# A new order for the pieces of a windowed-attention stage, a minimum for the sink columns, and sink remainders on GpSimd

## The chip, the cores and the metric

The kernel runs on one core of a Trainium2 chip. A time is the device time of one execution in microseconds (us); the kernel before has a median of 281.07 us over three runs (279.21, 281.07 and 281.68). Five engines work side by side, each through its own queue in program order: TensorE (PE) multiplies and transposes, VectorE (DVE), ScalarE (ACT) and GpSimd (POOL) work on tiles, and SyncE (SP) mostly starts transfers (DMA). An instruction that waits for another engine holds up everything behind it in its own queue.

## The reference

Three stages follow one another. The change is in the first one.

```python
def _attn_ref(q, k, v, n_sink, window):          # 4 batches, 8 heads, 768 tokens, 64 wide
    scores = scale * np.matmul(q, k.transpose(0, 1, 3, 2))
    keep = (pos[None, :] < n_sink) | ((rel >= 0) & (rel < window))   # n_sink = 4, window = 128
    scores = np.where(keep, scores, -1000000000.0)
    a = np.exp(scores - np.max(scores, axis=-1, keepdims=True))
    a = a / (np.sum(a, axis=-1, keepdims=True) + 1e-09)
    return np.matmul(a, v)
...
x = _moe_ref(...)     # a soft mixture of 8 experts over the 3072 tokens
return _moe2_ref(...) # each token through its one best expert
```

A token attends to the 128 tokens up to itself and to the first four tokens, the sink. All data are 32-bit floats.

## The kernel before, in words

**Units.** Two heads form a pair; there are 16 pairs. A pair has six blocks of 128 tokens and is worked in three units of two blocks, so there are 48 units. A unit u goes through twelve pieces, each a function `emit_...`:

- S (PE, L220): scores of two blocks for two heads into one of two PSUM tiles `sc0`, `sc1`. The tile of unit u is free again when E of unit u-2 has read it.
- M (DVE, L235): one predicated copy that folds the previous block's keys into the window. L (DVE, L243, L244): the row maximum; in a pair's first unit also L246, which puts the sink columns of the first block out of play by a predicated copy of `negs` under the mask `m_dup`.
- E (ACT, L257): four exponentials with row sums. R (DVE, L262, L263): the reciprocals. N (POOL, L267): the normalization.
- G (POOL, L275 to L277): the sink probabilities into the tile `st`, as a rounded part and a remainder. T (PE, L286): four transposes. C (ACT, L291): out of PSUM. A, B, D (POOL, L297 to L304): the triangles of the window into `pt`.

**Pairs.** A pair also has its own pieces: v0 (ACT, L310) rounds the sink values of `v` into `vst`, and v1 (DVE, L315) puts their remainder beside it; s and k (PE L320, DVE L326) spread the sink probabilities; P0 to P8 (PE, L333 to L341) multiply by `v`, into `xa` and `xb`; x (ACT, L346, L348) brings the result to SBUF; X, y, f and l transpose it, store it by token in `xtok` (ACT, L375) and add up the next stage's logits. After every fourth pair, eight more steps (among them L405 and L417 on PE) fold a finished batch into the mixture.

**Transfers.** SP's queue starts a pair's loads of `qk` (L80, two buffers: pair p waits for the last S of pair p-2) and `v` (L85, three buffers: a load waits until the last P of an earlier pair has read its buffer), and between them the weights of the next stage, 1 MB at a time (L488).

**What sets the order.** Every piece gets a number, its unit plus a key from the table `KEYS` (by the piece's name, the pair modulo four, and the first and last pair), and the pieces are written out in the order of these numbers. Each engine's queue, SP's too, follows that order; the waits between engines come from the data and the buffers alone. The stages after attention, from L530 on, have an order of their own, and the change does not touch it.

Of the kernel before, what the change touches and what calls it, by code (L numbers as in the profile page):

```python
# [33 lines left out]
NX = 10  # L34
CAP = 128 + NX
NEG = -1.0e30


@with_exitstack
def kernel_body(ctx, tc, qkv, n_sink, window, phi, m1w, emb, tau, m2w1, m2w2, out):  # L40
# [71 lines left out]
    pool.affine_select(out=t_le_q, in_=ones, pattern=[[-1, 128]], compare_op=ALU.is_ge, fill=0.0, base=0, channel_multiplier=1)  # L112

    m_dup = const.tile([128, 2, 2, SINK], F32, name="m_dup")
    ov = ones[:, 0:8].rearrange("p (h s) -> p h s", h=2)
    pool.affine_select(out=m_dup[:, :, 0, :], in_=ov, pattern=[[0, 2], [-1, SINK]], compare_op=ALU.is_ge, fill=0.0, base=0, channel_multiplier=1)
    pool.affine_select(out=m_dup[:, :, 1, :], in_=ov, pattern=[[0, 2], [1, SINK]], compare_op=ALU.is_gt, fill=0.0, base=0, channel_multiplier=-1)
    negs = const.tile([128, 16], F32, name="negs")
    dve.memset(negs, NEG)

    bm = const.tile([96, 4], F32, name="bm")
    for c in range(3):
# [65 lines left out]

    emit_W(5)
    dve.memset(sc_b[1], 0.0)  # L190
    dve.memset(negs, NEG)
    s_t, p_t, pt_t, xt_t, xtok_b = {}, {}, {}, {}, {}
    rs_t, nm_t = {}, {}

# [42 lines left out]
    def emit_L(u):  # L237
        p, t = divmod(u, 3)
        mv = merged(s_t[u])
        nm = small.tile([128, 2, 2], F32, tag="nm", name="nm")  # L240

        mx = mv[:, :, :, 192]
        dve.tensor_reduce(mx, mv[:, :, :, 0:UW], axis=X, op=ALU.max, negate=True)  # L243
        dve.tensor_scalar(out=nm, in0=mx, scalar1=0.125, scalar2=None, op0=ALU.mult)  # L244
        if t == 0:
            dve.copy_predicated(mv[:, :, :, 128:UW], m_dup.bitcast(U32), negs.rearrange("p (h i s) -> p h i s", h=2, i=2))  # L246
        nm_t[u] = nm

    def emit_E(u):
# [62 lines left out]

    def emit_v1(p):
        vst = vst_t[p]
        dve.tensor_tensor(out=vst[64:96, :], in0=v_t[p][64:96, VW:], in1=vst.bitcast(F32)[64:96, :], op=ALU.subtract)  # L315

    def emit_s(p, half):
        if half == 0:
# [70 lines left out]
    def dispatch(b):  # L389
# [37 lines left out]
    NU = 3 * NPAIR  # L427
    wx = ExitStack()
    KEYS = {
# [41 lines left out]
    }  # L471
    n_exp, n_done = {}, {}
    disp = {}
# [1180 lines left out]
```

## Time and profile before

| | us |
|---|---|
| median of three runs | 281.07 |
| profiled execution, its own time | 281.05 |
| its span, first to last instruction | 279.3 |
| attention, first S to last f | 5.9 to 162.3 |

Busy time over the span: PE 262.2 us (94%), DVE 194.1 (69%), ACT 193.4 (69%), POOL 162.0 (58%). TensorE's granted clock is 0.993 of full speed on average. In the profile, a line gives a group of like instructions with their busy time and the mean length of one in ns; an "idle before" is time in which the engine had nothing to run before that instruction, with the instruction that ended the wait. A busy PE is modelled from the starts of pipelined matmuls, so it also contains their fill and drain.

### The profile page before, as it was taken

The page shows a single profiled execution, that of the slowest core. Times are in us where ns is not written, and L with a number is a line of the kernel's source. Part 1 is how long each engine was busy: PE and PEld are TensorE (multiplying, and loading weights), DVE is VectorE, ACT ScalarE, POOL GpSimd, SP SyncE. Part 2 cuts the span into 40 slices and gives each one's busy share as a digit, 9 for nine tenths or more (in the row PEclk, how much of TensorE's full clock was granted, in tenths as well). Part 3 has the DMA queues.
Part 4 walks back from the last instruction along what each step waited for, and adds up shares of the span by engine and source line. Part 5 has one row for each costly group of instructions (what it writes and reads, how often), then busy time and mean ns, then how long its engine had stood idle before and what let it go on. Part 6 is the DMA issues. An engine that isn't in the chain of part 4 may idle for free.

```text
span 279.3 us, 8848 instructions
## 1 busy us (share of the span) xinstructions
PE 262.2 (94%) x3257; PEld 166.3 (60%) x3257; DVE 194.1 (69%) x574; ACT 193.4 (69%) x679; POOL 162.0 (58%) x377
## 2 busy tenths in 40 slices
PE   7988999979999989999999999999999998999990
PEld 5654666555666655666556663334387675677880
DVE  6887888997878998789987243444435989664410
ACT  2677989869799797898987632310135999686981
POOL 3488999978889888899888640001202996020000
PEclk9999999999999999999999999999999999999997
DMA  7939976199383596768616398999139200025874
GB/s 222 329 123 409 391 281 220 19 402 392 93 314 118 204 419 260 277 235 310 253 82 228 111 408 333 427 429 419 60 123 393 87 1 1 2 75 137 313 284 175
DMA packets 15197, 65.37 MB, mean 234 GB/s; under 512 B 2736, under 2 KB 3248, under 8 KB 11568
## 3 DMA queue, kind: packets, MB, share of 16 engines
q1 hardware_dynamic: 13600, 63.77, 60.7%
q10 hardware_dynamic: 1392, 0.48, 0.8%
q8 instruction: 27, 0.44, 0.6%
q0 software_dynamic: 160, 0.52, 0.6%
q14 instruction: 18, 0.15, 0.2%
HBM read 58.48 MB, written 6.29 MB: 232 GB/s over the span
## 4 chain that ended last, share of the span: by engine, by line
PE 57%; DVE 16%; POOL 10%; DMA 6%; issue 5%; ACT 4%; SPq 0%; POOLq 0%; ACTq 0%; DVEq 0%
PE sc L220 5%; PE b L858 5%; POOL pr L267 5%; PE m L286 4%; PE xa L341 4%; PE b L834 4%; DVE sc L243 3%; PE b L1195 3%; PE b L1385 3%; PE m L358 3%; PE xb L341 3%; DMA out_dram<-ot 2%; PE m L365 2%; DVE sc L235 2%; PE m L417 2%
## 5 line engine op out<-in xcount | busy, mean ns | idle before, releaser
L257 ACT ACTIVATE pr<-sc,nm 128x132 f32<-128x132 f32 x192 | 68.7, 375 | 8.5 <-DVE rs L262 3.4
L267 POOL TENSOR_TENSOR pr<-pr,rs 128x528 f32<-128x528 f32 x48 | 51.5, 1073 | 21.3 <-DVE rs L263 16.4
L257 ACT ACTIVATION_READ_ACCUMULATOR pr<-sc,nm 128x1 f32 x192 | 40.4, 210 | 0.0
L220 PE MATMUL sc<-qk 64*32 64x164 f32 (+4 forms) x1536 | 36.6, 294 | 0.3 <-ACT pr L257 0.2
L235 DVE COPY_PREDICATED sc<-t_le_q,sc 128x512 f32<-128x512 uint32 x48 | 33.1, 689 | 3.6 <-PE sc L220 2.3
L291 ACT ACTIVATE raw<-m 128x512 f32<-128x512 f32 x48 | 29.0, 604 | 7.9 <-PE xb L320 4.3
L243 DVE TENSOR_REDUCE sc<-sc 128x4 f32<-128x528 f32 x48 | 33.7, 703 | 0.8
L286 PE MATMUL m<-ident,pr 128*128 128x128 f32 x192 | 30.2, 280 | 3.9 <-ACT xtok L375 2.8
L297 POOL TENSOR_SCALAR_AFFINE_SELECT pt<-raw 128x512 f32<-128x512 f32 x48 | 30.6, 638 | 1.9 <-ACT raw L291 1.9
L341 PE MATMUL xa<-pt,v 128*64 128x256 f32 (+1 forms) x256 | 30.3, 360 | 0.0
L286 PEld LDWEIGHTS m<-ident,pr 128*128 128x128 f32 x192 | 21.4, 141 | 12.0 <-POOL pr L267 4.3
L220 PEld LDWEIGHTS sc<-qk 64*32 64x32 f32 x1536 | 21.2, 106 | 10.5 <-issue 4.4
L341 PEld LDWEIGHTS xa<-pt,v 128*64 128x64 f32 x256 | 15.4, 136 | 8.4 <-issue 4.3
L813 POOL CAST scr<-scr 128x256 fp32r<-128x256 f32 x6 | 2.4, 402 | 30.7 <-DVE scr L809 30.0
L304 POOL TENSOR_SCALAR_AFFINE_SELECT pt<-raw 128x256 f32<-128x256 f32 x48 | 19.6, 408 | 0.0
L341 PE MATMUL xb<-pt,v 128*64 128x128 f32 (+1 forms) x192 | 18.9, 314 | 0.0
L1172 POOL TENSOR_TENSOR w2h<-w2t,ones 128x512 fp32r<-128x512 f32 x8 | 8.3, 1043 | 15.4 <-PE b L1022 15.4
L375 ACT ACTIVATE xtok<-m 128x512 f32<-128x512 f32 (+1 forms) x32 | 15.7, 499 | 2.0 <-PE m L358 1.7
L341 PEld LDWEIGHTS xb<-pt,v 128*64 128x64 f32 x192 | 11.6, 136 | 7.3 <-POOL st L277 2.5
L358 PE MATMUL m<-ident,xt 128*128 128x128 f32 x96 | 15.9, 276 | 0.0
L1204 ACT ACTIVATE junk<-b 128x512 f32<-128x512 f32 (+1 forms) x26 | 14.8, 568 | 0.7 <-PE b L1195 0.3
L1385 PE MATMUL b<-w2c,hm 128*128 128x512 f32 x45 | 14.7, 400 | 0.0
(328 smaller groups left out, 571.2 us busy)
## 6 DMA issues: line engine op xcount, KB each, us to landing
w<-in_m1w_dram SPq DMA_DIRECT2D x19, 1024.0 KB, 8.2
qk<-in_qkv_dram SPq DMA_DIRECT2D x15, 780.0 KB, 4.4
w<-in_m1w_dram SPq DMA_DIRECT2D x4, 2048.0 KB, 12.8
v<-in_qkv_dram SPq DMA_DIRECT2D x16, 448.0 KB, 4.9
out_dram<-ot SPq DMA_DIRECT2D x19, 256.0 KB, 2.9
x<-in_m1w_dram SPq DMA_DIRECT2D x4, 1024.0 KB, 8.5
w1t<-in_m2w_dram SPq DMA_DIRECT2D x4, 512.0 KB, 5.2
w2t<-in_m2w_dram SPq DMA_DIRECT2D x4, 512.0 KB, 8.9
```

The costliest lines, as they stand in the source:

```text
L220: pe.matmul(sc[r0:r0 + 32, h, o + lo:o + hi], lhsT=lhsT, rhs=qk[hp:hp + 64, k0 + lo:k0 + hi], start=True, stop=True)
L235: dve.copy_predicated(mv[:, :, :, 0:128], mk.to_broadcast([128, 2, 2, 128]), bv[:, :, :, 124:252])
L243: dve.tensor_reduce(mx, mv[:, :, :, 0:UW], axis=X, op=ALU.max, negate=True)
L257: act.activation(out=pr[:, h, i2, :], in_=mv[:, h, i2, 0:UW], func=AF.Exp, bias=nm[:, h, i2:i2 + 1], scale=0.125, accum_out=sm[:, h, i2, 0:1])
L267: pool.tensor_tensor(out=pr, in0=pr, in1=sm.rearrange("p h (i o) -> p h i o", o=1).to_broadcast([128, 2, 2, UW]), op=ALU.mult)
L286: pe.transpose(ps[:, h, i2, :], pr[:, h, i2, 0:128], ident)
L291: act.activation(out=raw, in_=tp_t.pop(u), func=AF.Copy)
L297: pool.affine_select(out=pt[:, :, :, 0, :], in_=raw_t[u], pattern=[[0, 2], [0, 2], [1, 128]], compare_op=ALU.is_ge, fill=0.0, base=0, chan ...
L304: pool.affine_select(out=pt_t[u][:, :, 0, 1, :], in_=raw_t[u][:, :, 1, :], pattern=[[0, 2], [-1, 128]], compare_op=ALU.is_gt, fill=0.0, ba ...
L341: pe.matmul(o[64 * h:64 * h + 64, c0:c0 + 128 * (l1 - l0)], lhsT=v[:, j, h, :], rhs=mv[:, h, 128 * l0:128 * l1], start=False, stop=last, s ...
L358: pe.transpose(ps[:, 128 * t:128 * t + 128], xt[:, 128 * (t0 + t):128 * (t0 + t) + 128], ident)
L1385: pe.matmul(y, lhsT=a, rhs=b, start=(k == 0), stop=(k == 3))
```

## The change

Three edits. (1) `KEYS` has new numbers, so pieces, and loads among them, stand in another order on every engine. (2) The tile `m_dup` no longer holds 0 and 1 but -1e30 where a sink column is to be masked and 3e38 elsewhere, and a `tensor_tensor` with `min` takes the place of the predicated copy; `negs` and its two memsets are gone, and POOL gets one memset. (3) v1 goes from DVE to POOL. The number of matmuls, of other instructions and of loads is otherwise the same.

```diff
+BIG = 3.0e38
...
     m_dup = const.tile([128, 2, 2, SINK], F32, name="m_dup")
-    ov = ones[:, 0:8].rearrange("p (h s) -> p h s", h=2)
-    pool.affine_select(out=m_dup[:, :, 0, :], in_=ov, pattern=[[0, 2], [-1, SINK]], compare_op=ALU.is_ge, fill=0.0, base=0, channel_multiplier=1)
...
-    negs = const.tile([128, 16], F32, name="negs")
-    dve.memset(negs, NEG)
+    pool.memset(m_dup, NEG)
+    pool.affine_select(out=m_dup[:, :, 0, :], in_=m_dup[:, :, 0, :], pattern=[[0, 2], [-1, SINK]], compare_op=ALU.is_ge, fill=BIG, base=0, channel_multiplier=1)
...
-            dve.copy_predicated(mv[:, :, :, 128:UW], m_dup.bitcast(U32), negs.rearrange("p (h i s) -> p h i s", h=2, i=2))
+            dve.tensor_tensor(out=mv[:, :, :, 128:UW], in0=mv[:, :, :, 128:UW], in1=m_dup, op=ALU.min)
...
-        dve.tensor_tensor(out=vst[64:96, :], in0=v_t[p][64:96, VW:], in1=vst.bitcast(F32)[64:96, :], op=ALU.subtract)
+        pool.tensor_tensor(out=vst[64:96, :], in0=v_t[p][64:96, VW:], in1=vst.bitcast(F32)[64:96, :], op=ALU.subtract)
...
-        "T@3": (2.984, 2.2177, 1.8544,), "C@3": (3.2592, 2.8973, 2.1591,), ...
+        "T@3": (2.5712, 2.2359, 2.0133,), "C@3": (3.0669, 2.2451, 2.1058,), ...
```

What the numbers do is seen in the queues. Three places, each before and then with the change. The number behind a tile's name only tells tiles of one name apart.

**Place A, SP's queue near its start, before.** `qk_277` and `qk_286` are the loads of pairs 2 and 3, `v_102`, `v_296` and `v_344` those of pairs 1, 2 and 3.

```order
L85 DMA v_102<-in_qkv_dram 128x896
L488 DMA w0_273<-in_m1w_dram 128x2048
L80 DMA qk_277<-in_qkv_dram 128x1560
L80 DMA qk_286<-in_qkv_dram 128x1560
L85 DMA v_296<-in_qkv_dram 128x896
L488 DMA w0_273<-in_m1w_dram 128x2048
L488 DMA w1_320<-in_m1w_dram 128x2048
L85 DMA v_344<-in_qkv_dram 128x896
```

The same place with the change: `qk_270` and `qk_276` are pairs 2 and 3, `v_273` is pair 3 and `v_278` pair 2.

```order
L86 DMA v_102<-in_qkv_dram 128x896
L485 DMA w1_232<-in_m1w_dram 128x2048
L485 DMA w0_237<-in_m1w_dram 128x2048 x2
L81 DMA qk_270<-in_qkv_dram 128x1560
L86 DMA v_273<-in_qkv_dram 128x896
L81 DMA qk_276<-in_qkv_dram 128x1560
L86 DMA v_278<-in_qkv_dram 128x896
```

Three weight loads instead of one now stand ahead of pair 2's `qk`, the third `v` load follows it at once, and pair 3's `qk` no longer stands between.

**Place B, SP's queue at pairs 6 and 7, before.** `qk_606` and `v_891` are pair 6, `qk_810` and `v_1026` pair 7.

```order
L80 DMA qk_606<-in_qkv_dram 128x1560
L80 DMA qk_810<-in_qkv_dram 128x1560
L85 DMA v_891<-in_qkv_dram 128x896
L488 DMA w2_582<-in_m1w_dram 128x2048
L488 DMA w3_987<-in_m1w_dram 128x2048
L85 DMA v_1026<-in_qkv_dram 128x896
```

With the change: `qk_317` and `v_353` are pair 6, `qk_344` and `v_319` pair 7, `qk_360` and `v_399` pair 8.

```order
L81 DMA qk_317<-in_qkv_dram 128x1560
L86 DMA v_319<-in_qkv_dram 128x896
L81 DMA qk_344<-in_qkv_dram 128x1560
L86 DMA v_353<-in_qkv_dram 128x896
L81 DMA qk_360<-in_qkv_dram 128x1560
L485 DMA w1_232<-in_m1w_dram 128x2048
L86 DMA v_399<-in_qkv_dram 128x896
```

Every `qk` is now followed by one `v`; no two `qk` loads stand side by side. The same holds at pairs 10 and 11.

**Place C, PE's queue at the last two units of pair 7 (units 22 and 23), before.** L417 is the batch's fold, L341 the products with `v`.

```order
L335 MATMUL xb_1219<-pss_1329,vst_1126 128x256
L286 MATMUL m_1379<-ident_119,pr_1312 128x128 x4
L417 MATMUL m_1384<-xtok_682,et_sb_1337 32x512 x6
L341 MATMUL xb_1219<-pt_1308,v_469 64x256 x2
L341 MATMUL xb_1219<-pt_1308,v_469 64x128 x2
L341 MATMUL xb_1219<-pt_1261,v_469 64x128 x2
L320 MATMUL xa_1403<-ident_119,st0_135 96x128
L358 MATMUL m_1413<-ident_119,xt_1186 128x128 x4
L220 MATMUL sc0_166<-qk_810 32x164 x16
L333 MATMUL xa_1403<-pss_1411,vst_1188 128x512
L286 MATMUL m_1449<-ident_119,pr_1364 128x128 x4
L220 MATMUL sc1_167<-qk_810 32x164 x16
```

The same place with the change (the row before its first is unit 21's S):

```order
L333 MATMUL xb_1230<-pss_1356,vst_1052 128x256
L284 MATMUL m_1393<-ident_119,pr_1284 128x128 x4
L415 MATMUL m_1400<-xtok_619,et_sb_1349 32x512 x6
L339 MATMUL xb_1230<-pt_1313,v_313 64x128 x2
L339 MATMUL xb_1230<-pt_1381,v_313 64x128 x2
L339 MATMUL xb_1230<-pt_1381,v_313 64x256 x2
L318 MATMUL xa_1428<-ident_119,st0_138 96x128
L356 MATMUL m_1440<-ident_119,xt_1212 128x128 x4
L218 MATMUL sc0_169<-qk_344 32x164 x16
L218 MATMUL sc1_170<-qk_344 32x164 x16
L356 MATMUL m_1493<-ident_119,xt_1212 128x128 x2
```

The scores of units 22 and 23 now stand back to back, where a product, transposes and a spread stood between them. The same holds at units 34 and 35; before, only units 46 and 47 stood so.

## Rows read from the trace of the kernel before

**Rows 1.** Busy time by stretch: length, each engine's (xinstructions), PE clock, DMA, GB/s.

```profile
5.86:24.80 18.94, 16.45 (x295) 10.50 (x294) 15.32 (x47) 12.46 (x56) 12.96 (x31) 1.00 0.78 265
24.80:62.10 37.30, 34.49 (x634) 22.66 (x635) 33.34 (x86) 31.47 (x130) 33.46 (x84) 1.00 0.73 274
62.10:99.40 37.30, 36.33 (x623) 23.01 (x624) 31.37 (x86) 32.06 (x132) 31.88 (x76) 1.00 0.64 235
99.40:136.70 37.30, 36.67 (x626) 23.31 (x626) 32.70 (x89) 32.77 (x135) 32.77 (x81) 1.00 0.75 276
136.70:163.00 26.30, 25.74 (x332) 15.86 (x330) 16.64 (x47) 19.72 (x75) 20.51 (x53) 1.00 0.52 196
163.00:279.30 116.30, 108.18 (x746) 67.76 (x744) 60.55 (x200) 63.48 (x154) 27.68 (x40) 0.98 0.55 212
```

**Rows 2.** The same view for the warm-up matmuls of L187 alone, PE and PEld.

```profile
5.86:24.80 18.94, 5.03 (x19) 3.09 (x18) 1.00 0.78 265
```

**Rows 3.** Timeline of PE: start, us, instruction, idle before it and its releaser.

```profile
25.02 0.29 PE L320 MATMUL xa<-ident,st 128*96 128x128 f32 x1 [1.22 <-POOL st L276]
...
62.04 0.63 PE L286 MATMUL m<-ident,pr 128*128 128x128 f32 x4 [2.05 <-ACT xtok L375]
...
99.34 0.63 PE L286 MATMUL m<-ident,pr 128*128 128x128 f32 x4 [0.77 <-ACT xtok L375]
```

**Rows 4.** Timeline of ACT, the waits of v0 for a load of v.

```profile
24.13 0.31 ACT L310 ACTIVATE vst<-v 96x128 fp32r<-96x128 f32 x1 [1.38 <-DMA v<-in_qkv_dram]
...
60.83 0.31 ACT L310 ACTIVATE vst<-v 96x128 fp32r<-96x128 f32 x1 [2.44 <-DMA v<-in_qkv_dram]
...
98.14 0.31 ACT L310 ACTIVATE vst<-v 96x128 fp32r<-96x128 f32 x1 [1.16 <-DMA v<-in_qkv_dram]
```

**Rows 5.** Timeline of SP's queue: start and us of the issues, merged where like ones follow.

```profile
11.21 7.99 SPq L80 DMA_DIRECT2D qk<-in_qkv_dram  x2
19.24 0.83 SPq L85 DMA_DIRECT2D v<-in_qkv_dram  x1
...
45.23 9.25 SPq L80 DMA_DIRECT2D qk<-in_qkv_dram  x2
54.58 0.37 SPq L85 DMA_DIRECT2D v<-in_qkv_dram  x1
```

**Rows 6.** Lines L246 and L315: count, shortest, median and longest in ns.

```profile
L246 DVE COPY_PREDICATED sc<-m_dup,negs x16: 182/400/700, 8.5 to 144.5; 128x16 f32<-128x16 uint32 x16
...
L315 DVE TENSOR_TENSOR vst<-v,vst x16: 282/396/1220, 10.7 to 153.4; 32x128 fp32r<-32x128 f32 x16
```

**Rows 7.** Timeline of DVE and of POOL at 56.43 us.

```profile
56.43 1.22 DVE L315 TENSOR_TENSOR vst<-v,vst 32x128 fp32r<-32x128 f32 x1
...
56.43 1.07 POOL L267 TENSOR_TENSOR pr<-pr,rs 128x528 f32<-128x528 f32 x1
```

**Rows 8.** Groups by line: count, busy us, mean ns, idle before and its releasers.

```profile
L257 ACT ACTIVATE pr<-sc,nm 128x132 f32<-128x132 f32 x192 | 68.7, 375 | 8.5 <-DVE rs L262 3.4 <-DVE nm L244 2.7 <-DVE sc L246 1.6
L267 POOL TENSOR_TENSOR pr<-pr,rs 128x528 f32<-128x528 f32 x48 | 51.5, 1073 | 21.3 <-DVE rs L263 16.4 <-PE xa L320 2.4 <-ACT raw L291 1.0
...
L243 DVE TENSOR_REDUCE sc<-sc 128x4 f32<-128x528 f32 x48 | 33.7, 703 | 0.8
L235 DVE COPY_PREDICATED sc<-t_le_q,sc 128x512 f32<-128x512 uint32 x48 | 33.1, 689 | 3.6 <-PE sc L220 2.3 <-issue 0.7
...
L277 POOL TENSOR_TENSOR st<-pr,st 128x16 fp32r<-128x16 f32 x48 | 10.6, 221 | 0.0
```

**Rows 9.** Chain that ended last, near 70 us: start, us, what.

```profile
68.63 1.85 PE m L417 x12
70.48 1.02 PE xb L341 x12
```

**Rows 10.** Waits from 62.1 to 99.4 us: total, times, longest.

```profile
POOL pr L267 <- DVE rs L263: 3.6, 6, 0.8
```

**Rows 11.** The page's transfer rate in 40 equal slices of 7 us.

```profile
GB/s 222 329 123 409 391 281 220 19 402 392 93 314 118 204 419 260 277 235 310 253 82 228 111 408 333 427 429 419 60 123 393 87 1 1 2 75 137 313 284 175
```

More of the change, by code (lines that the diff above doesn't have):

```diff
@@ L114, in kernel_body @@
     m_dup = const.tile([128, 2, 2, SINK], F32, name="m_dup")
-    ov = ones[:, 0:8].rearrange("p (h s) -> p h s", h=2)
-    pool.affine_select(out=m_dup[:, :, 0, :], in_=ov, pattern=[[0, 2], [-1, SINK]], compare_op=ALU.is_ge, fill=0.0, base=0, channel_multiplier=1)
-    pool.affine_select(out=m_dup[:, :, 1, :], in_=ov, pattern=[[0, 2], [1, SINK]], compare_op=ALU.is_gt, fill=0.0, base=0, channel_multiplier=-1)
-    negs = const.tile([128, 16], F32, name="negs")
-    dve.memset(negs, NEG)
+    pool.memset(m_dup, NEG)
+    pool.affine_select(out=m_dup[:, :, 0, :], in_=m_dup[:, :, 0, :], pattern=[[0, 2], [-1, SINK]], compare_op=ALU.is_ge, fill=BIG, base=0, channel_multiplier=1)
+    pool.affine_select(out=m_dup[:, :, 1, :], in_=m_dup[:, :, 1, :], pattern=[[0, 2], [1, SINK]], compare_op=ALU.is_gt, fill=BIG, base=0, channel_multiplier=-1)
     bm = const.tile([96, 4], F32, name="bm")
@@ L190, in kernel_body @@
     dve.memset(sc_b[1], 0.0)
-    dve.memset(negs, NEG)
     s_t, p_t, pt_t, xt_t, xtok_b = {}, {}, {}, {}, {}
```

81 rows, old and new, of the table KEYS are left out of this document.

## The prediction

> **What bounds the kernel now.** I read the busy time by stretch first, to see where the change can act. Attention runs from 5.86 us (first S) to 162.3; the table [rows 1] cuts it into the filling of the pipeline, three periods of 37.30 us (four pairs, 12 units each) and a drain. In the second and third period PE is busy 36.33 and 36.67 of 37.30 us, in the first 34.49 (no batch is folded there, which costs 2.1 us of PE elsewhere, so its work is the smaller). DVE, ACT and POOL are at 31 to 33.5. So from 24.8 us on PE sets the pace, and all that a better order can give back is PE's idle time: 37.30 - 34.49 = 2.81, 0.97, 0.63 and, in the drain, 26.30 - 25.74 = 0.56, together 4.97 us. The filling is different: of 18.94 us PE is busy 16.45, but 5.03 of these are warm-up matmuls [rows 2], so there the latency from piece to piece counts. The last 116.30 us are later stages, which keep their order and shift as a whole.
>
> Next, PE's timeline for its idle spots. Three stand out [rows 3]: 1.22 us at 25.02, 2.05 at 62.04 and 0.77 at 99.34, together 4.04. Two are waits for ACT's xtok. The first is put down to a POOL cast, but the matmul there also needs ACT to have read xa of the pair before, and POOL had long been done. ACT's timeline shows the cause of all three: just before each, ACT stood at v0 for a load of v, for 1.38, 2.44 and 1.16 us [rows 4], with x and xtok queued behind it.
>
> Why is v late? SP's queue [rows 5]: at 11.21 and at 45.23 two qk loads follow one another, and the second waits for the last S of the pair before, so the merged issue takes 7.99 and 9.25 us. The load of v behind it leaves only at 19.24 and 54.58, though its buffer was free earlier (at the start it had never been used). The pattern of 45.23 repeats at pairs 10 and 11.
>
> **The change, part by part.**
>
> *The loads.* In places A and B every qk is followed by one v, and the waits of neighbours in the queue now come in the order in which PE reaches them: last S of a pair, last P of the pair three back in load order, next S. With no v behind a qk that waits 8 us, v0 finds its data. At place B, the load of pair 6 can leave with the last P of pair 4, some three units of 37.30/12 = 3.1 us before its v0 in the new order. This takes away the three PE waits: -1.22 - 2.05 - 0.77 = -4.04. They lie wholly on the path, since PE is the bound.
>
> *The new order.* It can open new waits or close old ones. What is left of PE's idle time after 24.8 us without these waits is 4.97 - 2.05 - 0.77 - 0.22 (the end of the first) = 1.93, so at best another -1.9. For the worst I take place C. The second of two S in a row waits for E of unit 21, and PE stands until then. From the end of unit 21's S that takes M 0.69, L 0.70, E four times 0.375 [rows 8] and handovers, about 3.3; a C ahead of E on ACT adds some 0.5. So at most 3.8. PE has between the two: the fold 1.85 and six products 1.02 [rows 9], 2.87, and besides a whole S, a product, a spread and two groups of transposes. If these took nothing, PE would wait 0.9 at each of the two places; since they are some forty matmuls against the fold's twelve, I take it as covered; without the fold it would be near the edge. In the filling, the first s now stands behind v1 and A on POOL, and S of unit 4 leaves up to 0.7 us later; against that, PE has three of the products behind it before unit 6. I take +0.4 for all new waits, with ends -1.9 and +2.
>
> *v1 on POOL.* It leaves DVE, where sixteen took a median of 396 ns and up to 1220 [rows 6]. The slow one at 56.43 began with POOL's normalization and ended just after it [rows 7]: the two exclude one another. This is what the Trainium skill says ("SBUF — State Buffer", section "SBUF: two separate sides"): VectorE with two SBUF inputs and GpSimd share one port pair under an exclusive lock. The trace agrees (1.22 us against 0.28 alone). On POOL, 128 elements lie between 16 (221 ns) and 528 (1073 ns) [rows 8]; by a straight line 0.22 + 112 x 0.852/512 = 0.41 us. Four per period make 33.46 + 1.64 = 35.1, below PE's 36.7 with a fold, so they lie beside PE: nothing. The ends 0.22 and 1.07 give 34.3 and 37.7; at the upper one POOL is the bound. The skill speaks against this move: "GPSIMD Engine Reference" (introduction) calls GpSimd the wrong choice for elementwise work, VectorE being about twice as fast; twice 0.28 would be 0.56, POOL at 35.7, and the sum the same.
>
> *The minimum.* One DVE instruction on 16 elements for another, in the same place. The predicated copy took 182 to 700 ns; I take 0.18, its shortest, since one input now lies in PSUM and only one in SBUF. That saves up to 16 x 0.2 us of DVE, with v1 some 12 us in all, on an engine that is 4 to 6 us per period below PE. ACT waited for it 1.6 us in all [rows 8], not PE: nothing; ends -0.5 and, if it took the longest length each time, +0.5. The memset of m_dup on POOL falls into POOL's idle time before its first normalization: nothing. The weight loads that moved all end before the stage that needs them: nothing, but for the first three (rivals).
>
> **Sum.** From the profiled execution's own 281.05 (span 279.3; 0.02 below the median of 281.07): 281.05 - 4.04 + 0.4 = **277.4 us**. One per cent of 281.07, about what a measurement tells from no change, is 2.8 us, so the bounds are 278.26 and 283.88. Own range of this case: 276.0 to 278.9. Chance 0.52.
>
> **The rivals.**
>
> 1. *The waits are only handed on.* ACT reaches x and xtok in time, but the next latest piece stops PE a little later: N waits for R, S for E. For it: POOL's and ACT's many short waits (8.5 us before E, 21.3 before N over the kernel [rows 8]). Against: the third period has the same order without a v wait and runs with 0.63 us of idle PE. A third of the gain stays: 281.05 - 1.3 = 279.7. Chance 0.22.
>
> 2. *PE's floor.* The other 1.9 us go too: 281.05 - 4.04 - 1.9 = 275.1. For it: DVE loses 12 us of work and its stalls against POOL. Against: no order closes every handover. Chance 0.08.
>
> 3. *Weights ahead of pair 2* (place A). Before pair 2's qk has landed, 780 + 448 + 780 + 448 + 3 x 1024 + 780 KB and 81 KB of small loads must pass, 6.5 MB. The first slice moves 222 GB/s, 1.55 MB in 7 us [rows 11]. At the 419 of a busy slice the rest takes 11.8 us and is there at 18.7; at the 329 of the second slice it takes 15 us, until 21.9. Unit 6's S started at 20.6, so the slow rate costs 1.3 us: 278.7. Chance 0.08. In it and in rival 1, the load change does what it says and the gain is lost nearby.
>
> 4. *POOL becomes the bound: slower.* POOL's idle time is partly waiting for reciprocals, 3.6 us in the second period [rows 10]. If that latency stays while v1 lengthens POOL's chain, a period takes 33.46 + 1.64 + 3.6 = 38.7, that is 1.4 more than now, over 137.5 us (24.8 to 162.3) 3.7 times: +5.2. The filling keeps its 1.2: 285.0. It decides from a v1 of (36.7 - 33.46)/4 = 0.81 us on if the waits shrink, and at 0.41 already if they stay. Against: those waits exist because PE, upstream of E and R, is late; they shrink when POOL is late instead. Chance 0.10. By the skill's rule above (0.56 each) it would be 0.6 more per period.
>
> **Numbers.** Faster by over 1% (below 278.26): about 0.43 of case one's 0.52, all of rival 2, a little of rivals 1 and 3: 0.55. Slower: the larger part of rival 4 and a rest for order mishaps: 0.09. Same: 0.36. The range leaves out the lower half of rival 2 and most of rival 4: 275.3 to 281.8.
>
> **What the profile would show.** Right: no ACT wait at v0 for a v load behind 10 us; no issue of two qk loads over 7 us in SP's queue; PE idle below 0.8 us at any place after 25 us; the first period near 35 us of length with PE idle under 1 us; unit 7's S at about 24 instead of 25.23. v1 on POOL near 0.4 us, min near 0.18, no stretching to POOL's length. DVE busy about 182 us. Later stages again 116 us long. Wrong: a PE wait at units 23 and 35 for E (place C too tight); POOL above 36.5 us in a period with PE waiting for its normalization (rival 4); S of unit 6 waiting for qk (rival 3); or the same idle PE spread over many small waits (rival 1).

## The result and the profile after

The changed kernel has a median of 278.71 us over 16 runs (276.2 to 281.39), the kernel before 281.44 over 16 beside them. The ratio, changed over before, is 0.9892, with a 95% interval of 0.9863 to 0.9922: about 3 us less. The profiled execution took 277.48 us with a span of 275.7 (before 281.05 and 279.3). Some executions of most kernels here show a lower granted clock and take longer; the ratios leave out those that stand out, the medians do not.

The same cut of both kernels, by stretch: up to unit 7's S, from there to the last f, and the later stages. The columns are those of [rows 1]. First before:

```profile
0.00:25.23 25.23, 21.04 (x305) 13.82 (x305) 19.47 (x70) 14.37 (x59) 16.10 (x49) 1.00 0.75 254
25.23:161.73 136.50, 131.74 (x2193) 83.90 (x2192) 113.18 (x302) 115.37 (x467) 117.75 (x287) 1.00 0.67 247
161.73:279.30 117.57, 109.45 (x761) 68.58 (x761) 61.43 (x202) 63.70 (x155) 28.11 (x42) 0.98 0.56 215
```

Then after:

```profile
0.00:25.64 25.64, 20.97 (x301) 13.65 (x302) 18.30 (x66) 13.67 (x57) 15.78 (x47) 1.00 0.81 306
25.64:157.84 132.20, 130.24 (x2196) 83.59 (x2195) 104.48 (x289) 116.19 (x469) 124.74 (x306) 1.00 0.69 244
157.84:275.70 117.86, 109.44 (x761) 68.45 (x761) 61.60 (x202) 63.74 (x155) 28.14 (x42) 0.99 0.56 214
```

The filling lost 0.41 us, the middle gained 4.30, the later stages lost 0.29: together the 3.6 us of the span. In the middle TensorE's idle time fell from 4.76 to 1.96 us. It is also *busy* 1.5 us less, with the same work. This is not shorter matmuls. Groups of TensorE over one period of 12 units, unit 19's S to unit 31's (count, busy us, mean ns, idle before), before (59.20 to 97.78 us):

```profile
L220 PE MATMUL sc<-qk 64*32 64x164 f32 (+3 forms) x384 | 9.2, 294 | 0.0
L341 PE MATMUL xa<-pt,v 128*64 128x256 f32 (+1 forms) x64 | 7.7, 360 | 0.0
L341 PE MATMUL xb<-pt,v 128*64 128x128 f32 (+1 forms) x48 | 4.8, 314 | 0.0
```

And after (60.87 to 96.43 us):

```profile
L218 PE MATMUL sc<-qk 64*32 64x164 f32 (+3 forms) x384 | 9.0, 294 | 0.0
L339 PE MATMUL xa<-pt,v 128*64 128x256 f32 (+1 forms) x64 | 7.3, 360 | 0.0
L339 PE MATMUL xb<-pt,v 128*64 128x128 f32 (+1 forms) x48 | 4.5, 314 | 0.0
```

In these groups counts and mean lengths are the same and the busy time is less: a matmul starts more often before the modelled end of the one ahead of it. So a busy TensorE before contained short handovers that the timeline does not list as idle. The period as a whole, after:

```profile
60.87:96.43 35.56, 35.56 (x623) 22.94 (x623) 29.98 (x84) 32.00 (x132) 34.46 (x85) 1.00 0.73 262
```

TensorE is listed as busy for all of the 35.56 us, where the same 623 matmuls were busy 36.33 us before.

TensorE's idle spots from 20 us on, after (to be held against [rows 3]; 157.84 was there before too, at 161.73):

```profile
22.50 0.73 PE L218 MATMUL sc<-qk 64*32 64x36 f32 x32 [1.86 <-DMA qk<-in_qkv_dram]
33.98 0.32 PE L318 MATMUL xa<-ident,st 128*96 128x128 f32 x1 [0.20 <-POOL st L275]
35.80 0.79 PE L218 MATMUL sc<-qk 64*32 64x164 f32 x32 [0.23 <-ACT pr L255]
39.79 0.65 PE L339 MATMUL xa<-pt,v 128*64 128x256 f32 x4 [0.69 <-POOL pt L299]
149.68 0.32 PE L318 MATMUL xa<-ident,st 128*96 128x128 f32 x1 [0.26 <-POOL st L275]
157.84 0.63 PE L363 MATMUL m<-xt,phi_sb 128*32 128x256 f32 x6 [0.47 <-ACT xtok L373]
```

The three spots of [rows 3] are gone; nothing stands between 40 and 149 us, so place C made no idle spot either. A new one is at unit 6's S, which waits 1.86 us for pair 2's qk. In SP's queue, where [rows 5] had merged issues of 7.99 and 9.25 us, there stands now:

```profile
7.37 3.75 SPq L485 DMA_DIRECT2D w<-in_m1w_dram  x3
11.40 0.36 SPq L81 DMA_DIRECT2D qk<-in_qkv_dram  x1
11.81 0.44 SPq L86 DMA_DIRECT2D v<-in_qkv_dram  x1
...
47.29 0.33 SPq L81 DMA_DIRECT2D qk<-in_qkv_dram  x1
51.81 0.33 SPq L86 DMA_DIRECT2D v<-in_qkv_dram  x1
56.26 0.33 SPq L81 DMA_DIRECT2D qk<-in_qkv_dram  x1
59.97 0.33 SPq L86 DMA_DIRECT2D v<-in_qkv_dram  x1
```

Each load leaves by itself. On ACT, v0 waits for a load of v only once, for the first pair; the waits of [rows 4] have no successors. The two engine edits (counts; shortest, median and longest ns), beside [rows 6]:

```profile
L244 DVE TENSOR_TENSOR sc<-sc,m_dup x16: 182/182/183, 8.7 to 140.4; 128x16 f32<-128x16 f32 x16
...
L313 POOL TENSOR_TENSOR vst<-v,vst x16: 448/452/456, 12.2 to 147.1; 32x128 fp32r<-32x128 f32 x16
```

### The profile page after: what moved, and what is told of

Read it like the earlier page. It is cut to its first block, busy times and chain, and to the rows that moved or that the text cites. A ratio compares the mean times of both kernels' runs of the same rounds, so it can differ in the third digit from the quotient of the medians.

```text
span 275.7 us, 8854 instructions
## 1 busy us (share of the span) xinstructions
PE 260.6 (95%) x3257; PEld 165.7 (60%) x3257; DVE 184.4 (67%) x556; ACT 193.6 (70%) x679; POOL 168.7 (61%) x394
## 5 line engine op out<-in xcount | busy, mean ns | idle before, releaser
L339 PE MATMUL xa<-pt,v 128*64 128x256 f32 (+1 forms) x256 | 29.5, 361 | 0.7 <-POOL pt L299 0.7
L284 PE MATMUL m<-ident,pr 128*128 128x128 f32 x192 | 28.9, 276 | 0.6 <-POOL pr L265 0.6
L284 PEld LDWEIGHTS m<-ident,pr 128*128 128x128 f32 x192 | 22.0, 141 | 4.1 <-POOL pr L265 2.1
L339 PE MATMUL xb<-pt,v 128*64 128x128 f32 (+1 forms) x192 | 18.1, 315 | 0.0
L339 PEld LDWEIGHTS xb<-pt,v 128*64 128x64 f32 x192 | 10.7, 136 | 5.0 <-issue 3.8
```

The lines of the kernel that those rows point to most:

```text
L284: pe.transpose(ps[:, h, i2, :], pr[:, h, i2, 0:128], ident)
L339: pe.matmul(o[64 * h:64 * h + 64, c0:c0 + 128 * (l1 - l0)], lhsT=v[:, j, h, :], rhs=mv[:, h, 128 * l0:128 * l1], start=False, stop=last, s ...
```

## The experiments

Twelve runs were made, two of them repeats, in three groups with the kernel before among each (medians 281.58, 282.32 and 282.3). Across groups the ratios are compared, not the times. "Last f" is the end of attention.

### What do the loads give by themselves?

The kernel before, with one key changed, so that the v loads of pairs 2, 6 and 10 stand ahead of the next qk:

```diff
-"Lv@2": (-5.0602,),
+"Lv@2": (-6.1,),
```

> The kernel before with one number of the order table changed (Lv@2 from -5.06 to -6.1): in SP's queue the v load of pairs 2, 6 and 10 now stands ahead of the qk load of the pair after it. Nothing else moves on any engine. My theory (late v loads held ACT, and ACT held PE): the three ACT waits at v0 (1.38, 2.44, 1.16 us) and the three PE waits (1.22, 2.05, 0.77) are gone, and the kernel is 4.0 us faster, about 277.4 against 281.4, ratio near 0.986. Rival (the wait is only handed on to the next late piece): about 1.3 us faster, ratio near 0.995, with new PE waits within 10 us of the old places.

Measured: 278.38 us (277.85 to 279.05), ratio 0.9897 (0.9847 to 0.9947). All three v waits are gone. TensorE's larger idle spots from 50 to 100 us (two more have 0.25 and 0.17):

```profile
59.62 0.55 PE L286 MATMUL m<-ident,pr 128*128 128x128 f32 x3 [0.40 <-POOL pr L267]
96.80 0.66 PE L286 MATMUL m<-ident,pr 128*128 128x128 f32 x4 [0.41 <-POOL pr L267]
```

So of the 4.04 us about 2.9 arrive by the ratio (its interval spans 1.5 to 4.3), and in the profiled executions attention ends 2.31 us earlier (159.42 against 161.73). The rest is handed on: where 2.05 and 0.77 us went, the normalization is the next to be late, by 0.40. One number of the table is worth as much as the whole change.

### And the rest without the loads' help?

The new order alone: the kernel before with the new `KEYS`, while the predicated copy and v1 stay on VectorE. Of its diff, one line of the table:

```diff
-        "T@3": (2.984, 2.2177, 1.8544,), "C@3": (3.2592, 2.8973, 2.1591,), ...
+        "T@3": (2.5712, 2.2359, 2.0133,), "C@3": (3.0669, 2.2451, 2.1058,), ...
```

> The kernel before with the new order table alone: predicated copy and the sink remainders stay on VectorE. My theory (the order and its loads carry the whole gain, the two engine edits lie beside PE's work): as the changed kernel within 0.5 us, about 278.5, ratio near 0.989. Rival (the order was found for the lighter VectorE, and needs it): VectorE's 12 us come back on a path that the new order made tight, PE shows new waits for VectorE and most of the gain is lost, 280 or more.

Measured: ratio 1.0001 (0.9957 to 1.0044), nothing. **My theory fell here**: the loads stand in the better order, the three v waits are gone, and no time came of it. Its profiled execution (284.55 us) ran at a lower granted clock near 25 us (last section). What it shows beside that is a 2.56 us wait for pair 2's qk and, at a clock of 1.00, a period of 36.79 us (65.34 to 102.13) instead of 35.56.

The engine edits alone, in the old order:

```diff
-            dve.copy_predicated(mv[:, :, :, 128:UW], m_dup.bitcast(U32), negs...
+            dve.tensor_tensor(out=mv[:, :, :, 128:UW], in0=mv[:, :, :, 128:UW], in1=m_dup, op=ALU.min)
...
-        dve.tensor_tensor(out=vst[64:96, :], in0=v_t[p][64:96, VW:], ...
+        pool.tensor_tensor(out=vst[64:96, :], in0=v_t[p][64:96, VW:], ...
```

> The kernel before with the two engine edits alone (minimum in place of the predicated copy, sink remainders on GpSimd), in the old order. My theory: no change, 281.4 within 0.7 us, ratio 0.998 to 1.002; the three ACT waits for v stay, VectorE busy falls by 9 to 12 us. Rival (VectorE's stalls against GpSimd were on the path): 1.5 us faster or more. Rival (GpSimd, with 7 us more, sets the pace): 1.5 us slower or more.

Measured: ratio 1.0008 (0.9965 to 1.005), as expected. Neither part alone gives anything that can be told from noise, together they give 3 us. Two questions follow: what the filling costs, and why the new order needs the engine edits.

### The filling: three weight loads ahead of pair 2's qk

The changed kernel, its first three weight loads behind pair 2's qk and the v load that follows it:

```diff
         k = k[n % len(k)]
+        k = max(k, -10.5 - n) if f is load_half else k
         pieces.append((n + k, len(pieces), f, a))
```

> The changed kernel with the first three weight loads moved behind the loads of pair 2's qk and pair 3's v in SP's queue. My theory (they delayed pair 2's qk, so that PE waited 1.86 us before unit 6): that wait is gone, unit 7's scores start near 24 instead of 25.64, and the kernel is 1.5 to 1.9 us faster than the changed one, about 277.0, ratio to before near 0.983. Rival (the filling is bound by the chain of pieces anyway): PE waits elsewhere before 30 us, and the time stays at 278.7.

Measured: 276.07 us (274.87 to 276.38), ratio 0.9812 (0.9763 to 0.9861). It was run again, with the changed kernel, unaltered, in the same group:

> The changed kernel itself, on the same chip as the next one: 277.5 to 279 (ratio 0.985 to 0.993).

> The kernel with its first weight loads later, a second time and beside the changed kernel: 275.5 to 276.5, 2 to 3 us less than the changed kernel (the 1.86 us wait of unit 6 for its queries, and what the lower clock after it costs in some executions). If the gain seen before was the chip's and not the kernel's, both give the same time within 0.5 us.

Measured: the changed kernel 277.08 us, ratio 0.9891 (0.9843 to 0.9939); with the weights later 275.2 us (274.77 to 275.69), ratio 0.9799 (0.9748 to 0.985). The step is 1.9 us. The two have the same middle. The changed kernel:

```profile
0.00:25.58 25.58, 21.59 (x301) 14.12 (x301) 18.43 (x66) 13.65 (x57) 15.62 (x47) 1.00 0.86 307
25.58:157.72 132.14, 130.26 (x2196) 83.62 (x2195) 104.51 (x289) 115.94 (x469) 124.39 (x306) 1.00 0.70 244
```

With the weights later:

```profile
0.00:24.08 24.08, 21.28 (x301) 13.84 (x301) 18.19 (x65) 13.83 (x58) 15.16 (x47) 1.00 0.81 296
24.08:156.22 132.14, 130.25 (x2196) 83.61 (x2196) 104.64 (x290) 115.96 (x468) 124.96 (x306) 1.00 0.71 250
```

132.14 us in both; the 1.5 us lie before unit 7's S, where the wait for qk (1.33 us in this execution, 1.86 in the other) is gone. The rest of the 1.9 is not in these two traces. This kernel is faster than the kernel before and the changed one: the slowest of its six runs (275.69) lies below the fastest of the changed kernel's twelve beside it (276.28).

### Why the new order needs the engine edits

All three start from the kernel with its weights later, so that the wait for qk does not blur the answer. First v1 back on VectorE:

```diff
-        pool.tensor_tensor(out=vst[64:96, :], in0=v_t[p][64:96, VW:], ...
+        dve.tensor_tensor(out=vst[64:96, :], in0=v_t[p][64:96, VW:], ...
```

> The kernel with its first weight loads later (276.07 us, ratio 0.9812), with the sink remainder v1 back on VectorE; the minimum stays. In the traces so far a period of 12 units (4 pairs) in the middle lasts 35.56 us with the whole change, 36.79 with the new order alone (1.23 us more, with TensorE busy for 36.43 of it by the same 623 matmuls), 37.18 in the old order with the v loads swapped. Theory A (the new order pays only with a lighter VectorE, since VectorE's queue now stands ahead of TensorE's work): v1 is 4 instructions of 0.39 to 0.66 us per period on VectorE, so the period is 0.3 to 0.6 us longer than 35.56 and over some 3.5 periods the time is 277.1 to 278.2. Rival B (the order alone lost at the fill, through its 2.56 us wait for the queries and the lower clock after it, not in the periods): 276.1, period within 0.1 of 35.56.

Measured: 277.25 us (276.8 to 278.99), ratio 0.9852 (0.9794 to 0.991), period 36.06 us, the next one 36.36. Then the predicated copy back in place of the minimum:

```diff
-            dve.tensor_tensor(out=mv[:, :, :, 128:UW], in0=mv[:, :, :, 128:UW], in1=m_dup, op=ALU.min)
+            dve.copy_predicated(mv[:, :, :, 128:UW], m_dup.bitcast(U32), negs...
```

> The kernel with its first weight loads later, with the predicated copy over the sink columns back in place of the minimum; v1 stays on GpSimd. Theory A: the copy lies between the row maximum and the exponentials of every third unit (0.44 to 0.75 us against 0.18, so 0.3 to 0.6 us more on 4 units of a period), the larger part of the loss; period 36.2 to 36.6 and time 278.3 to 279.7. Rival B: 276.1, period within 0.1 of 35.56.

Measured: 276.79 us (275.3 to 277.52), ratio 0.9823 (0.977 to 0.9875), period 35.82 us: less than theory A wanted of it. The ratios of these two can't be told from the 0.9812 of the kernel that they start from; the periods can, which repeat there within 0.02 us. Then both, that is the two diffs together:

> The new order with its first weight loads later, and neither edit of an engine: predicated copy and v1 on VectorE as in the kernel before. The wait of unit 6 for its queries (2.56 us with the order alone) goes in both theories. Theory A: the period stays at 36.8, so 1.23 us times some 3.5 periods stay lost: 280.0 to 280.8 (ratio 0.995 to 0.998). Rival B: what the order alone lacked was the fill, so it comes to 276.1 to 277 (ratio 0.981 to 0.984).

Measured: 280.18 us (279.09 to 281.17), ratio 0.9934 (0.9901 to 0.9967), period 36.72 us. Theory A holds in sum: both edits back cost 1.16 us per period. By parts it had the wrong one as the larger: from unit 7's S to the last f, v1 alone costs 2.59 us, the copy alone 0.95, both 4.07 (134.73, 133.09 and 136.21 against 132.14). The waits over a period (total, times, longest), here with both back, 61.08 to 97.80 us:

```profile
POOL pr L268 <- DVE rs L264: 4.1, 6, 1.5
```

With v1 alone back (59.62 to 95.68 us):

```profile
POOL pr L265 <- DVE rs L261: 3.2, 5, 1.1
```

In the changed kernel and in the one with its weights later no such wait is among the first of the list; the largest with VectorE as releaser is 0.9 us in all (ACT for `rs`). Such a wait need not cost anything by itself: the kernel without v1 (below) has 2.2 us of it per period and loses none. The longest here lies behind place C, and there the loss is: of the 1.16 us, 0.55 lie between unit 24's S and unit 25's (76.58 to 80.69, 4.11 us against 3.56), in the next period too. VectorE's queue there, with both back:

```profile
72.05 0.39 DVE L316 TENSOR_TENSOR vst<-v,vst 32x128 fp32r<-32x128 f32 x1 [0.98 <-ACT vst L311]
...
73.36 0.67 DVE L236 COPY_PREDICATED sc<-t_le_q,sc 128x512 f32<-128x512 uint32 x1
74.06 0.72 DVE L244 TENSOR_REDUCE sc<-sc 128x4 f32<-128x528 f32 x1
74.81 0.16 DVE L245 TENSOR_SCALAR nm<-sc 128x4 f32<-128x4 f32 x1
75.01 0.51 DVE L316 TENSOR_TENSOR vst<-v,vst 32x128 fp32r<-32x128 f32 x1
75.55 0.70 DVE L236 COPY_PREDICATED sc<-t_le_q,sc 128x512 f32<-128x512 uint32 x1
76.28 0.72 DVE L244 TENSOR_REDUCE sc<-sc 128x4 f32<-128x528 f32 x1
77.03 0.16 DVE L245 TENSOR_SCALAR nm<-sc 128x4 f32<-128x4 f32 x1
77.11 0.41 DVE L327 TENSOR_TENSOR pss<-xb,bm 96x256 fp32r<-96x256 f32 x1
77.44 0.15 DVE L263 TENSOR_REDUCE rs<-sm 128x4 f32<-128x8 f32 x1
77.62 0.18 DVE L264 RECIPROCAL rs<-rs 128x4 f32<-128x4 f32 x1
```

GpSimd's normalization behind it:

```profile
77.95 1.07 POOL L268 TENSOR_TENSOR pr<-pr,rs 128x528 f32<-128x528 f32 x1 [1.47 <-DVE rs L264]
```

The two S that stand back to back give VectorE two masks and two maxima in a row, v1 stands between them, and the reciprocals come last. One v1 ahead of them costs more than its length: it holds VectorE's queue for 0.98 us until ScalarE has rounded the values (v0), with unit 22's mask behind it. GpSimd idles 1.47 us for the reciprocals, and TensorE's transposes get their input later. TensorE shows little of it as idle time (36.38 of 36.72 us busy); the rest of the loss is in the handovers, as in the kernel before.

In the old order the same edits, with the loads cured as in the first experiment, should then be worth nothing. The diff is that of the engine edits alone and

```diff
-"Lv@2": (-5.0602,),
+"Lv@2": (-6.1,),
```

> The kernel before with the v loads of pairs 2, 6 and 10 ahead of the next query and key load, and with both engine edits (minimum, v1 on GpSimd): the old order of the pieces stays. Theory (the engine edits are worth something only where the order leaves VectorE's queue as what TensorE waits for; the old order's waits end with GpSimd and ScalarE): 278.0 to 278.7 as without the edits (278.38). Rival (the edits are worth 3.7 us wherever the late loads are gone, as in the new order): 274.5 to 275.5, period about 36.0 instead of 37.18.

Measured: 278.42 us (277.56 to 279.71), ratio 0.9928 (0.9894 to 0.9961), in total no gain over the loads alone (0.9897, with an interval that overlaps). But the period did get shorter, 36.66 against 37.18 us, while attention ends at 159.11 against 159.42. TensorE's timeline shows two places that took back most of it:

```profile
28.51 0.87 PE L339 MATMUL xa<-pt,v 128*64 128x256 f32 x8 [0.27 <-POOL pt L302]
29.54 0.66 PE L284 MATMUL m<-ident,pr 128*128 128x128 f32 x4 [0.17 <-POOL pr L265]
...
153.31 0.50 PE L331 MATMUL xa<-pss,vst 96*128 96x512 f32 x1 [0.49 <-POOL vst L313]
```

Between unit 7's S and unit 9's, 5.73 us against 4.86, GpSimd works from 21 to 30 us without a listed wait and now has two v1 of 0.45 us in it; TensorE waits for what stands behind them. In the drain TensorE waits for v1 itself. So the theory came out in the total, not in its mechanism: in the old order too the edits are worth half a microsecond per period (1.16 in the new), and GpSimd's longer work at both ends takes most of that back.

### Which engine sets the period now?

The kernel with its weights later, with one more v1 per pair on GpSimd, written to a tile of its own:

```diff
+        pool.tensor_tensor(out=scr[64:96, :], in0=v_t[p][64:96, VW:], ...
         pool.tensor_tensor(out=vst[64:96, :], in0=v_t[p][64:96, VW:], ...
```

> The kernel with its first weight loads later, with one more v1 on GpSimd per pair (the same 32 x 128 subtraction, written to a tile that nobody reads, ahead of the real one). GpSimd is busy for 34.47 of a period of 35.56 us, four more of 0.45 us make 36.27. If GpSimd became the bound as soon as it is fuller than TensorE (the rival of the prediction in which GpSimd becomes the bound), the period is at least 36.3 and the time 2.5 us or more above 276.07, so 278.6 to 280. If its busy time overstates what it is needed for, or its backlog is worked off in the later stretch in which it is idle, 276.1 to 277.

Measured: 283.32 us (282.4 to 284.55), ratio 1.0057 (1.0026 to 1.0088): slower than the kernel before, and by more than I expected. The period:

```profile
61.97:99.60 37.63, 36.29 (x623) 22.91 (x623) 30.13 (x83) 32.18 (x132) 36.05 (x89) 1.00 0.71 248
```

Four times 0.45 us is 1.8, the period grew by 2.07 (the next one by 1.83): all of it passes on, though GpSimd is listed as busy for 36.05 of 37.63. So its last 1.1 us of 35.56 in the change were no reserve.

And none at all:

```diff
-        pool.tensor_tensor(out=vst[64:96, :], in0=v_t[p][64:96, VW:], ...
+        pass
```

> The kernel with its first weight loads later (276.07 us) without v1 at all: the sink rows of v keep their rounded value, the subtraction of the remainder is left out on every engine. With one v1 more per pair the period grew from 35.56 to 37.63 us (four times 0.45 is 1.8), with v1 on VectorE to 36.06. Theory (TensorE, busy for the whole of 35.56, sets the period, and GpSimd is only just short of it): period 35.5, time 275.5 to 276.1. Rival (GpSimd sets it already, TensorE's busy time merely filling up): the period falls by up to 1.8 to some 34, the time to 270 to 274.

Measured: 638.61 us for the whole, which says nothing of v1: without the remainders, later stages took a branch that no other kernel here takes (L1079 to L1081, 384 matmuls each). Attention lies ahead of that and can be read:

```profile
57.95:93.50 35.55, 35.55 (x624) 22.95 (x623) 29.96 (x84) 31.97 (x132) 32.49 (x81) 1.00 0.74 262
```

Of GpSimd's waits in that stretch:

```profile
POOL pr L265 <- DVE rs L261: 2.2, 5, 0.8
```

With 2 us less on GpSimd the period stays at 35.55, and GpSimd waits instead. So GpSimd does not set it but stands just behind. What is left is TensorE, the only engine without a gap (VectorE 29.96, ScalarE 31.97). That 35.55 is the least these matmuls can take is not shown: 36.33 was no floor either.

## Why the prediction was right, and where it was not

The forecast was 277.4 us against the profiled 281.05; the profiled execution after took 277.48, and the median of 278.71 lies in the range. The size is right. That it is right to 0.1 us is luck: one term was too small by 1.32 us, another of 1.57 the other way was missing.

- *The loads, -4.04.* Right in mechanism: the idle spots of [rows 3] and the waits of [rows 4] are all gone. In size somewhat too large where it was tried by itself: in the old order the loads alone give about 2.9 us.
- *All new waits, +0.4.* Too small. TensorE's idle time up to the last f fell from 8.95 (4.19 + 4.76) to 6.63 (4.67 + 1.96), by 2.32, not 4.04: new waits took 1.72 net, and 1.86 of them are one wait, that of unit 6's S for pair 2's qk. This is rival 3, to which I gave 0.08. Its working was near (qk there between 18.7 and 21.9, by its own terms 18.8 and 22.0, against a start at 20.6; TensorE stood from 20.64 and resumed at 22.50), but I gave the slow rate too little weight, and even that was not slow enough.
- *What an order can give back.* "All that a better order can give back is PE's idle time" failed. A busy TensorE contained handovers: the same matmuls took 36.33 us of a period and now 35.56, over the middle 131.74 and 130.24. This term, -1.57 with the filling's -0.07, was not in the sum. It happens to pay for the new waits that were set too small. With the later stages' +0.29: -4.04 + 1.72 - 1.57 + 0.29 = -3.6.
- *Engine edits at nothing.* In the old order true in the total (ratios 1.0008 alone, 0.9928 against 0.9897 with the loads cured), but by cancellation; wrong in the new one: there both together are worth 0.9934 against 0.9812. This is the same miss as the one above: in the new order TensorE is busy for 36.4 us of a period without the edits (36.43 and 36.38), for 35.56 with both. The failing sentence is that they act "on an engine that is 4 to 6 us per period below PE". VectorE's mean load was no measure of it; behind two S in a row the reciprocals stood at the end of its queue.
- *Rival 1.* It shows in small where the loads are cured alone: 0.40 us for the normalization in each period. In the change no such wait is left behind 40 us.
- *Rival 2, PE's floor.* Its 1.9 us did not go: up to the last f 1.96 us of the middle's idle time are left, 1.23 in the first period and 0.73 in the drain. Between, from 40 to 149 us, there is no idle spot, and leaving v1 out does not shorten the period; the further gain came out of the busy time, which the rival did not price.
- *Rival 4, GpSimd as the bound.* It did not happen, for the reason given: its waits for the reciprocals, 3.6 us in [rows 10], shrink to 0.2, and come back as 2.2 when v1 is left out. But the margin was thinner than the 1.6 us that I saw: one v1 more per pair costs 2.07 us a period. The Trainium skill's warning ("GPSIMD Engine Reference", introduction: elementwise work about twice as slow there) was half borne out: 452 ns against 282 at best and 396 at the median on VectorE, and leaving it out does not shorten the period.
- *Signs.* v1 0.45 us against 0.41, the minimum 0.182 against 0.18, no stretching of either, VectorE busy 184.4 against 182, later stages as before. Unit 7's S came at 25.64 and not at 24, which was the sign of rival 3; with the weights later it came at 24.08. The first period, from unit 7's S to unit 19's, has 35.23 us, near the 35 of the forecast, but TensorE idles 1.23 us in it and not under 1 (34.00 busy).
- *Place C.* TensorE did not wait there, as I argued; what the place loads is VectorE's queue, which I had not followed.

## What to carry to other kernels

- Do not take the busy time of a period's matmuls for its floor: equal counts and equal mean lengths with a different busy sum mean hidden handovers.
- When an order is changed, follow each engine's queue at the places that move, also the lightly loaded ones; an edit that saves nothing in one order can be what makes another one pay, so try parts together and apart.
- Before the first loop, write the loads in the order in which the engines need them, large ones that nobody waits for last.

## What the runs showed of the hardware

After the 2.56 us wait in the order alone, TensorE ran at a lower granted clock. Its windows:

```profile
20.00:24.50 4.50, 1.94 (x37) 1.04 (x34) 1.74 (x6) 1.69 (x9) 3.03 (x9) 0.78 0.80 317
24.50:30.00 5.50, 5.50 (x58) 3.58 (x57) 3.10 (x9) 2.44 (x8) 3.22 (x8) 0.56 0.02 7
```

The S behind that wait took 1.23 us, where the same 32 matmuls take 0.73. A clock of 0.56 over 5.5 us is mostly the lower of the two levels, 1.2 GHz. In the changed kernel's two profiled executions the same wait was 1.86 and 1.33 us long, and the clock stayed at 1.00. What decides it was not tried.

The minimum, with one input in PSUM and one in SBUF, took 182 or 183 ns each time, where the predicated copy, with mask and data in SBUF, took 182 to 700 ([rows 6]). Its longest, at 41.97 us, ended at 42.67, just after GpSimd's normalization (41.57 to 42.63). This agrees with the Trainium skill ("SBUF — State Buffer", section "SBUF: two separate sides"), by which a VectorE instruction with two SBUF inputs and a GpSimd instruction that reads SBUF exclude one another; v1 on VectorE, which has two SBUF inputs, took up to 1220.
